# The last 128 output rows of a fused attention and MLP kernel, computed as 384 and then 128 columns

## The chip, the cores and the metric

The kernel runs on one core of a Trainium2 chip. The metric is the device time of one execution in microseconds (us), as the median of several runs. A profiled execution is a separate one: it gives the trace, in which all times count from the first instruction (the span), and it has a time of its own.

## What is computed

The reference is an attention with forget gates, and an MLP on its result:

```python
scores = (q @ k.T) / sqrt(D)                 # per batch and head, S = 576, D = 64
decay  = cum[:, None] - cum[None, :]         # cum: running sum of log(clip(f))
attn   = softmax(where(causal, -1e9, scores + decay))
x      = (attn @ v)                          # heads side by side: 4608 rows of 512
h      = x @ w_in                            # 512 -> 2048
out    = (h - tanh(h)) @ w_out               # 2048 -> 512, float32
```

There are 8 batches of 8 heads. The output is 4608 rows of 512 float32 numbers.

## The kernel before

The work of the attention is cut into 32 pairs of heads. The MLP is cut into NU = 9 row blocks of UW = 512 rows. For each row block there are 32 steps, in a list `mlp` (L429): 16 steps `mlp1` (L386), each of which computes 128 of the 2048 hidden columns for 512 rows and puts them through `gate` (L379), and 16 steps `mlp2` (L413). The order on every engine is written out by hand (`manual_schedule`, L103): `slot` (L456) weaves the MLP's steps in between the attention's, and when the attention is over, L585 runs the steps that are left, one after the other.

`mlp2` multiplies the gated hidden values by `w_out`. Step s handles rows m = s // 4 of the row block (128 rows) and a quarter of the 16 hidden tiles: four matmuls of 128x512 (L419) that accumulate in one PSUM tile `ops`. The tile is taken at the first quarter (L416), from a pool `ps_m` with three buffers, which `gate`'s inputs share. After the fourth quarter, ScalarE copies the 128x512 float32 result from PSUM to an SBUF tile `ost` (L423; pool `tmp`, two buffers), and SP issues one store of 128 rows of 2048 bytes (L425).

So at the very end of the program, TensorE runs 64 matmuls of L419 for four blocks of 128 rows. The last block's copy and store come after the last matmul. The program ends (in the profile, L609) when SP has seen the semaphores of all stores. SP's stores use eight of these semaphores in turn.

The engines touched by the change, with what each still has to do at the end: TensorE only L419; ScalarE only the copies of L423; VectorE nothing after the last `gate` (L383); SP only the stores of L425.

Of the kernel before, what the change touches and what calls it, by code (L numbers as in the profile page):

```python
# [8 lines left out]
FP32 = mybir.dt.float32  # L9
# [13 lines left out]
def kernel(  # L23
# [10 lines left out]
    nc = tc.nc  # L34
    P = 128
# [3 lines left out]
    DM, DFF = moe_w_in.shape  # L39
# [9 lines left out]
    NFT = DFF // P  # L49
    NCH = DM // P  # L50
    UW = 512
    SB = UW // 2
    NU = NT // UW
# [7 lines left out]
    tmp = ctx.enter_context(tc.tile_pool(name="tmp", bufs=2))  # L61
# [4 lines left out]
    ps_m = ctx.enter_context(tc.tile_pool(name="ps_m", bufs=3, space=PSUM))  # L66

    win = wpl.tile([P, NCH, DFF], FP16)
    wout = wpl.tile([P, NFT, DM], FP16)
# [148 lines left out]
    E, XN, GT, M2, AV = {}, {}, {}, {}, {}  # L218
# [167 lines left out]
    def mlp1(u, s):  # L386
# [23 lines left out]
        for m in range(UW // P):  # L410
            GT[(u, s, m)] = gt[:, m * P:(m + 1) * P]

    def mlp2(u, s):  # L413
        m, part = divmod(s, 4)
        if part == 0:
            M2[u] = ps_m.tile([P, DM], FP32, tag="m", name="ops")  # L416
        ops = M2[u]
        for ft in range(part * 4, part * 4 + 4):
            nc.tensor.matmul(out=ops, lhsT=GT[(u, ft, m)], rhs=wout[:, ft, :],  # L419
                             start=(ft == 0), stop=(ft == NFT - 1))  # L420
        if part == 3:
            ost = tmp.tile([P, DM], FP32, tag="ost", name="ost")
            nc.scalar.activation(out=ost, in_=ops, func=AF.Copy)  # L423
            r0 = u * UW + m * P
            nc.sync.dma_start(out=out[r0:r0 + P, :], in_=ost)  # L425

    pairs = [(b, c) for b in range(B) for c in range(NPAIR)]

    mlp = [(fn, u, s) for u in range(NU) for fn in (mlp1, mlp2) for s in range(NFT)]  # L429
    done = [0]  # L430

# [182 lines left out]
```

## Time and profile before

| what | us |
|---|---|
| unprofiled runs: median of 3 (lowest, highest) | 357.48 (357.40, 357.85) |
| the profiled execution's own time | 358.57 |
| its span, first to last instruction | 356.86 |
| TensorE busy | 346.6 (97%) |
| ScalarE busy | 224.5 (63%) |
| VectorE busy | 191.9 (54%) |
| GpSimd busy | 150.9 (42%) |

The profiled execution is 1.71 us longer than its span, and 1.09 us longer than the unprofiled median. The busy times are shares of the whole span, over stages with different limits, so for a change at the end only the last microseconds tell. In the groups of instructions, a line gives the source line, the engine, the operation, what it writes and reads with its shape, the count, then the busy time in us and the mean length of one in ns, and after the second bar the idle time before, with what ended it. In the order of time, a line gives the start and the length in us. Two matmuls that follow each other overlap in these lengths, so their pace is read from the starts.

### The profile page before, as it was taken

How to read it: one execution, taken by the hardware profiler on the slowest of the kernel's cores; microseconds unless marked ns; L12 is line 12 of the kernel's file. 1: busy time of each engine (PE TensorE's matmuls, PEld its weight loads, DVE VectorE, ACT ScalarE, POOL GpSimd, SP SyncE). 2: the span in 40 equal slices, each digit the busy share in tenths (PEclk: the TensorE clock that was granted, in tenths of full speed). 3: DMA queues.
4: the chain of work that ended last, by engine and by line, in shares of the span. 5: the costliest groups of instructions: out<-in, count | busy, mean ns of one | idle time of the engine just before them, and what ended most of it. 6: DMA issues, size and time to landing. Idle time of an engine off the chain costs nothing.

```text
span 356.9 us, 7839 instructions
## 1 busy us (share of the span) xinstructions
PE 346.6 (97%) x2987; PEld 200.9 (56%) x2987; DVE 191.9 (54%) x358; ACT 224.5 (63%) x413; POOL 150.9 (42%) x291
## 2 busy tenths in 40 slices
PE   7989998999999999999999999999999999999995
PEld 3878886555555555555557865555555554444442
DVE  7667788439851676157714681478137513802810
ACT  4686976357855885588657865786568734714721
POOL 8973523554476527662776277632222210000000
PEclk9999999999999999999999999999999999999999
DMA  9999999999199969999999979991220012011002
GB/s 93 144 207 185 206 187 150 133 148 184 24 110 171 144 98 99 154 142 129 69 151 184 119 53 152 156 145 31 85 74 18 15 64 75 2 59 60 2 38 80
DMA packets 148439, 38.70 MB, mean 108 GB/s; under 512 B 137330, under 2 KB 142770, under 8 KB 148402
## 3 DMA queue, kind: packets, MB, share of 16 engines
q0 software_dynamic: 100128, 18.36, 70.2%
q1 hardware_dynamic: 48194, 19.77, 28.5%
q8 instruction: 23, 0.38, 0.4%
q14 instruction: 14, 0.11, 0.1%
q10 hardware_dynamic: 80, 0.08, 0.1%
HBM read 36.85 MB, written 9.44 MB: 130 GB/s over the span
## 4 chain that ended last, share of the span: by engine, by line
PE 92%; ACT 3%; DVE 2%; DMA 1%; issue 1%; ACTq 0%
PE ops L419 35%; PE hps L407 30%; PE ps L332 10%; PE av L360 7%; PE hps L393 3%; PE ps L274 2%; PE t L255 1%; PE av L287 1%; PE t L234 1%; ACT e L279 1%; ACT th L381 1%; ACT e L341 1%; DVE gt L383 1%; DMA lf<-in_f_dram 1%; PE ps L277 1%
## 5 line engine op out<-in xcount | busy, mean ns | idle before, releaser
L419 PE MATMUL ops<-wout,gt 128*128 128x512 f16 x576 | 140.3, 378 | 0.0
L383 DVE TENSOR_TENSOR gt<-hps,th 128x512 f16<-128x512 f32 x144 | 99.1, 690 | 60.3 <-ACT th L381 59.7
L341 ACT ACTIVATE e<-ps 128x512 f16<-128x512 f32 x168 | 99.2, 594 | 47.4 <-PE ps L332 40.0
L407 PE MATMUL hps<-XR,win 128*128 128x512 f16 (+1 forms) x576 | 125.6, 355 | 0.2
L381 ACT ACTIVATE th<-hps 128x512 f32<-128x512 f32 x144 | 86.0, 597 | 29.0 <-PE hps L407 22.9
L351 POOL TENSOR_SCALAR_AFFINE_SELECT e<-e 128x128 f16<-128x128 f16 x144 | 49.0, 340 | 104.6 <-ACT e L341 102.0
L419 PEld LDWEIGHTS <-gt 128*128 128x128 f16 x576 | 51.9, 97 | 52.8
L407 PEld LDWEIGHTS <-win 128*128 128x128 f16 x576 | 52.3, 97 | 44.3 <-issue 0.5
L332 PE MATMUL ps<-QT,KT 67*128 67x512 f16 (+1 forms) x336 | 70.9, 277 | 1.9 <-ACT e L341 1.9
L332 PEld LDWEIGHTS <-KT 67*128 67x128 f16 x336 | 32.8, 98 | 33.4
L423 ACT ACTIVATE ost<-ops 128x512 f32<-128x512 f32 x36 | 21.5, 597 | 39.2 <-PE ops L419 39.2
L366 DVE TENSOR_SCALAR rs<-av 128x10 f32<-128x10 f32 x28 | 4.6, 164 | 68.3 <-PE av L360 68.2
L86 POOL DMA_DIRECT2D vn<-in_v_dram x40 | 34.1, 856 | 9.6 <-PE ps L332 3.6
L360 PEld LDWEIGHTS <-e 128*128 128x128 f16 x784 | 28.1, 97 | 5.5
L360 PE MATMUL av<-vn,e 128*128 128x65 f16 x784 | 29.1, 193 | 0.0
L86 POOL DMA_DIRECT2D qn<-in_q_dram x25 | 21.2, 850 | 10.8 <-PE ps L332 6.2
L368 DVE TENSOR_TENSOR xn<-av,rs 128x640 f16<-128x640 f32 x28 | 23.1, 825 | 1.0
L86 POOL DMA_DIRECT2D kn<-in_k_dram x25 | 21.4, 855 | 1.4 <-issue 1.2
L279 ACT ACTIVATE e<-ps 128x512 f16<-128x512 f32 x25 | 14.4, 596 | 5.3 <-PE ps L277 3.9
L393 PE MATMUL hps<-XR,win 128*128 128x256 f16 x128 | 16.6, 272 | 0.5 <-DVE gt L383 0.5
L243 DVE COPY QT<-t 64x576 f16<-64x576 f16 x12 | 9.6, 803 | 6.8 <-PE t L234 5.2
L274 PE MATMUL ps<-QT,KT 67*128 67x128 f16 (+1 forms) x120 | 11.6, 214 | 1.5 <-ACT e L279 0.8
(79 smaller groups left out, 210.1 us busy)
## 6 DMA issues: line engine op xcount, KB each, us to landing
out_dram<-ost SPq DMA_DIRECT2D x36, 256.0 KB
vn<-in_v_dram POOLq DMA_DIRECT2D x32, 128.0 KB, 5.8
qn<-in_q_dram POOLq DMA_DIRECT2D x24, 128.0 KB, 4.1
kn<-in_k_dram POOLq DMA_DIRECT2D x24, 128.0 KB, 4.5
win<-in_moe_w_in_dram POOLq DMA_DIRECT2D x2, 1024.0 KB, 11.0
wout<-in_moe_w_out_dram POOLq DMA_DIRECT2D x4, 512.0 KB, 11.9
XR<-xn SPq DMA_TRANSPOSE x56
qn<-in_q_dram POOLq DMA_DIRECT2D x1, 576.0 KB, 16.8
```

The lines of the kernel that those rows point to most:

```text
L86: nc.gpsimd.dma_start(out=dst[0:pn, n, h0:h1, 0:D], in_=src[b, h0:h1, n * P:n * P + pn, :].rearrange("h p d -> p h d"))
L332: nc.tensor.matmul(out=ps[:, col:col + n], lhsT=KT[b % 2][0:D + 3, h, j * P:(j + 1) * P], rhs=QT[b % 2][0:D + 3, h, i0:i0 + n], start=True ...
L341: nc.scalar.activation(out=e[:, lo:hi], in_=ps[:, lo:hi], func=AF.Exp, scale=qscale)
L351: nc.gpsimd.affine_select(out=view, in_=view, compare_op=ALU.is_ge, fill=0.0, base=0, pattern=pat, channel_multiplier=-1)
L360: nc.tensor.matmul(out=av[:, a, ib, :], lhsT=E.pop((b, 2 * c + a, j, ib)), rhs=vn[b % 2][:, j, 2 * c + a, 0:D + 1], start=(j == 0), stop=( ...
L368: nc.vector.tensor_tensor(out=xn.rearrange("p i (a d) -> p a i d", a=2), in0=av[:, :, :, 0:D], in1=rs.to_broadcast([P, 2, NJ, D]), op=ALU. ...
L381: nc.scalar.activation(out=th, in_=hps, func=AF.Tanh, scale=-1.0)
L383: nc.vector.tensor_tensor(out=gt, in0=hps, in1=th, op=ALU.add)
L393: nc.tensor.matmul(out=hps[:, w * SB:(w + 1) * SB], lhsT=win[:, ci, ft * P:(ft + 1) * P], rhs=XR[:, ci, t * SB:(t + 1) * SB], start=(ci == ...
L407: nc.tensor.matmul(out=hps[:, o:o + n], lhsT=win[:, ci, s * P:(s + 1) * P], rhs=XR[:, ci, t:t + n], start=(ci == 0), stop=(ci == NCH - 1))
L419: nc.tensor.matmul(out=ops, lhsT=GT[(u, ft, m)], rhs=wout[:, ft, :], start=(ft == 0), stop=(ft == NFT - 1))
L423: nc.scalar.activation(out=ost, in_=ops, func=AF.Copy)
```

## The change

The last block of 128 rows (m = 3 of the last row block) is no longer handled by the four quarters of `mlp2`. A new function computes it at the first of them, and the other three do nothing. It first accumulates columns 0 to 383 over all 16 hidden tiles, copies them with VectorE and stores them, and then does the same for columns 384 to 511. Each part takes its own `ops` and `ost` buffer. The weights of TensorE (the gated tile) are loaded once for each matmul, so 32 times instead of 16. All other blocks are as before.

```diff
+    def last_rows(u, m):
+        r0 = u * UW + m * P
+        for c0, c1 in ((0, 3 * P), (3 * P, DM)):
+            ops = ps_m.tile([P, DM], FP32, tag="m", name="ops")[:, 0:c1 - c0]
+            for ft in range(NFT):
+                nc.tensor.matmul(out=ops, lhsT=GT[(u, ft, m)], rhs=wout[:, ft, c0:c1],
+                                 start=(ft == 0), stop=(ft == NFT - 1))
+            ost = tmp.tile([P, DM], FP32, tag="ost", name="ost")[:, 0:c1 - c0]
+            nc.vector.tensor_copy(out=ost, in_=ops)
+            nc.sync.dma_start(out=out[r0:r0 + P, c0:c1], in_=ost)
+
     def mlp2(u, s):
         m, part = divmod(s, 4)
+        if u == NU - 1 and m == UW // P - 1:
+            if part == 0:
+                last_rows(u, m)
+            return
         if part == 0:
             M2[u] = ps_m.tile([P, DM], FP32, tag="m", name="ops")
```

## The prediction

> **What bounds the kernel now.** I read the page's chain first, then the same chain in order of time over the last 22 us, then the end slice by slice. On the page, TensorE is busy 97% of the span and its clock was granted in full in every slice, so work that ends earlier on another engine is worth nothing unless it stands after the last matmul.
>
> ```profile
> PE   7989998999999999999999999999999999999995
> PEclk9999999999999999999999999999999999999999
> ...
> PE 92%; ACT 3%; DVE 2%; DMA 1%; issue 1%; ACTq 0%
> ```
>
> The change touches only the last rows, so the end of the chain matters (start us, length us, what):
>
> ```profile
> 334.81 4.53 PE hps L407 x21
> 339.34 13.83 PE ops L419 x64
> 353.17 0.03 ACTq L423
> 353.19 0.04 issue
> 353.24 0.60 ACT ost L423
> ```
>
> The reader is to see that TensorE runs its last 64 matmuls without a gap, 13.83 / 64 = 0.216 us each. The last row block is the last 16 of them; by the trace its first starts at 349.53 and its last ends at 353.15. ScalarE then copies the whole 128x512 result, 353.24 to 353.83, alone. SP issues the store at 353.86. The stretches after that show (length, TensorE, weight loads, VectorE, ScalarE, GpSimd, clock, DMA share, GB/s):
>
> ```profile
> 353.20:353.90 0.70, 0.00 (x0) 0.00 (x0) 0.00 (x0) 0.60 (x1) 0.00 (x0) 1.00 0.00 0
> 353.90:354.60 0.70, 0.00 (x0) 0.00 (x0) 0.00 (x0) 0.00 (x0) 0.00 (x0) 1.00 0.00 0
> 354.60:355.60 1.00, 0.00 (x0) 0.00 (x0) 0.00 (x0) 0.00 (x0) 0.00 (x0) 1.00 0.67 262
> 355.60:356.90 1.30, 0.00 (x0) 0.00 (x0) 0.00 (x0) 0.00 (x0) 0.00 (x0) 1.00 0.00 0
> ```
>
> So the 3.70 us after the last matmul are a series: 0.09 handover, 0.60 copy, 0.03 handover, 0.83 from issue to the first packet, 0.83 of packets (354.69 to 355.52), 0.35 until the last count of the store's semaphore (355.87), and 0.99 of closing instructions. SP's waits name that store as what the program's end hangs on:
>
> ```profile
> SPq L609 <- DMA out_dram<-ost: 1.2, 1, 1.2
> ```
>
> All in all the span is 356.86 and the profiled execution 358.57, thus 1.71 outside. The unprofiled median is 357.48 (357.4 to 357.85), 1.09 below the profiled one. I work out a difference inside the span and take it off the median.
>
> **TensorE.** Removed: 16 matmuls of 512 columns. Added: 16 of 384 and then 16 of 128, with 16 more weight loads. No row has 384, so I take the pace from three widths (start, length, then the form):
>
> ```profile
> 18.36 0.39 PE L308 MATMUL x<-id,xn 128*128 128x128 f16 x4
> 18.59 0.22 PE L274 MATMUL ps<-QT,KT 67*128 67x128 f16 x1
> ...
> 27.02 1.04 PE L393 MATMUL hps<-XR,win 128*128 128x256 f16 x8
> 27.90 0.19 PE L274 MATMUL ps<-QT,KT 67*128 67x64 f16 x1
> ```
>
> Starts count, since lengths overlap: (18.59 - 18.36) / 4 = 0.057 at 128 columns (0.0555 as the trace's median), (27.90 - 27.02) / 8 = 0.110 at 256, 0.216 at 512. These lie on a line of 0.0004175 per column plus some 0.002; 384 gives 0.1625. So 16 x (0.1625 + 0.0555) = 3.49 against 16 x 0.216 = 3.46: **0.03 us later**. The last 128-column matmul starts at 349.53 + 16 x 0.1625 + 15 x 0.0555 = 352.97 and lasts 0.22 (the same rows): 353.19. The bounds are 0 and the case in which every weight load (97 ns mean at L419) sets the pace in the narrow pass: 16 x (97 - 55.5) = 0.66. I take the low end, since the 65-column matmuls of L360 start every 29 ns while their weight loads also last 97 ns: loads overlap each other.
>
> Both new accumulations take PSUM buffers that ScalarE emptied at 343.4 and 346.9, so neither waits.
>
> **The copies.** The wide part is ready at 349.53 + 15 x 0.1625 + 0.33 (length between those of 320 and 448 columns, 0.30 and 0.35) = 352.30. VectorE has been idle since 340.7. A float32 copy out of PSUM at these sizes isn't in the trace. The nearest rows are:
>
> ```profile
> L383 DVE TENSOR_TENSOR gt<-hps,th 128x512 f16<-128x512 f32 x144 | 99.1, 690 | 60.3 <-ACT th L381 59.7
> L366 DVE TENSOR_SCALAR rs<-av 128x10 f32<-128x10 f32 x28 | 4.6, 164 | 68.3 <-PE av L360 68.2
> L309 DVE COPY XR<-x 128x512 f16<-128x512 f16 x4 | 1.7, 414 | 0.0
> ```
>
> The two float32 rows give (690 - 164) / 502 = 1.05 ns per column: 0.56 us for 384, 0.29 for 128. By the 2-byte copy (414 at 512 columns, 280 at 256) 128 would be 0.21; the far end is 0.60, as long as today's copy. I take 0.29, from the float32 rows. The wide copy runs 352.39 to 352.94, beside the narrow matmuls. The narrow one is free to start at 353.19 + 0.09 = 353.27, because VectorE has been done 0.33 earlier, and ends at 353.56: 0.27 before today's.
>
> The narrow copy also gains a wait: with two buffers for ost it must wait until the store of the block before last has read its buffer. That store was issued at 350.41 and landed at 352.41, 0.86 before it is needed. Nothing is queued behind the copy on VectorE but the end of the program; SP waits for it.
>
> **The stores.** SP issues the wide store at 352.97, busy 0.33 and then some 0.05 of semaphore work, so it is free at 353.35, before the narrow issue at 353.59. First packets come 0.83 after the issue. A store is 128 packets over 16 engines, 8 each; 2048-byte packets last 84 ns (8 x 84 = 0.67, plus 0.15 of uneven starts = the 0.83 seen). SP's queue has 1024-byte packets of 46 ns and 256-byte ones of 18, though no stores: so 1536 bytes gives 65 and 512 bytes 27. Wide packets run 353.80 to 354.47. Narrow ones could start at 354.42, when most engines are just done: 354.42 + 0.15 + 8 x 0.027 = 354.79. Bounds for 512 bytes: 18 and 84 ns, or -0.07 and +0.46.
>
> Landing 0.35 later gives 355.14 instead of 355.87: 0.73 earlier. After the landing SP goes through its last semaphores at some 0.06 each; the store has moved from the last but one to the last of them, which takes one step off: **0.79 in all**. The terms: -0.31 shorter copy, +0.04 matmuls (0.03 and rounding), -0.46 shorter packets, -0.06 closing step. 357.48 - 0.79 = **356.7 us**, 0.22% less. About 0.2% (0.71 us) is what a measurement of this kernel can tell from no change, so the forecast lies close to that bound.
>
> **Rivals.**
>
> *Weight loads pace the narrow pass.* Each narrow matmul then takes 97 ns, the end comes 0.66 later, and the saving shrinks to 0.13: 357.35. For it: the trace's 128-column runs are only 4 to 8 long. Against it: those runs, and 30 loads in a row at L360 without strain. Chance 0.07. The Trainium skill, page "TensorE: Matmul & The Clock Gate", section "Back-to-back issue gap", speaks for it: in streams of weight load and matmul it states about 81 ns at 128 columns. By that the sum would be 16 x 25 = 0.41 smaller, an estimate of about 357.1; the rows at 56 ns here don't agree, nor does 216 at 512, where it states about 131.
>
> *Small packets cost as much as big ones.* If 512 bytes take 84 ns, the narrow packets follow the wide ones on each engine: 354.47 + 0.67 = 355.14, landed 355.49, closing 0.06: a saving of 0.44, 357.05. For it: time per byte rises from 0.041 ns at 2048 to 0.070 at 256. Against it: 18 ns for 256 bytes shows that no such floor exists on this queue for other transfers. Chance 0.18, partial forms included. The Trainium skill, page "Perfetto Trace Analysis", section "DMA Optimizations", warns that DMAs under 2 KB have significant overhead per transfer, without a figure.
>
> *The second store waits for the first* (the slower side). If the narrow store's first packet can't come before 0.83 after the wide one has landed (354.47 + 0.35 = 354.82), it starts at 355.65, its packets end at 356.02, it lands at 356.37, and the end is 0.44 later than today: 357.9. It decides once the extra delay passes 0.79. Against it: two stores issued at 78.75 and 79.37 landed at 82.25 and 82.94, so the second came 0.68 after the first and not 2. Chance 0.05.
>
> *The split is not what runs.* The built instruction order shows 16 matmuls of 384, 16 of 128, two copies and two stores, last on each engine, and all before unchanged. No chance left.
>
> **How the numbers follow.** The forecast case has the remaining 0.70, with a spread of some 0.25 from the copy, the packets and the three runs; a little over two thirds of that lies beyond 0.71 saved. Faster 0.50, within 0.45, slower 0.05. The range takes in the small-packet case at one end (357.05 and a tenth for the runs) and the low bounds of copy and packets at the other (-0.08, -0.07, and the runs' spread): 356.35 to 357.2.
>
> **What would show it.** Right: the last matmul near 353.2, a copy of 0.29, packets of about 27 ns, a landing near 355.1. Wrong: narrow matmuls above 60 ns apart, packets of 512 bytes near 84 ns, an idle gap between the last matmul and the narrow copy above 0.2 (the ost buffer), or a narrow issue that stands more than 0.05 behind its copy (SP still busy).

## The result and the profile after

The changed kernel takes 356.81 us (median of 22 runs, 356.44 to 358.56) against 357.75 (22 runs, 357.24 to 360.98). The ratio is 0.9974, with a 95% interval of 0.9963 to 0.9985. So it is faster, by 0.93 us as the ratio has it; the interval stays clear of no change, but it reaches across the 0.2% that the prediction named as its bound. By time alone it stays open on which side of that bound the change lies.

The profiled execution of the changed kernel has a span of 354.73 and took 356.44. Its span is 2.13 below that of before, but most of this isn't the change's: 1.39 of it is there by the 12th us, and it then stays at 1.39 in every later stage. The first scores (L274) started between 7.88 and 8.90 in the profiled executions of this study, although nothing ahead of them differs. What the change does is therefore read from the end stretch alone: from the start of ScalarE's copy of the block before last, which all versions have, to the end of the span. Before it is 356.855 - 349.783 = 7.07, after it is 354.728 - 348.394 = 6.33. The difference is **0.74 us**. The landmark in the timeline of the kernel before (start us, length us, engine, line, operation, shapes; in brackets the engine's idle time before it and what ended that):

```profile
349.78 0.60 ACT L423 ACTIVATE ost<-ops 128x512 f32<-128x512 f32 x1 [2.90 <-PE ops L419]
```

The chain of the kernel after, in order of time (start us, length us, what):

```profile
337.95 10.36 PE ops L434 x48
348.31 3.51 PE ops L418 x32
351.81 0.04 DVEq L421
351.85 0.04 issue
351.89 0.29 DVE ost L421
```

TensorE still runs into its last matmul without a gap. The 0.60 of ScalarE that stood behind it has become 0.29 of VectorE. The timeline of the kernel after, in the same stretch:

```profile
348.39 0.60 ACT L438 ACTIVATE ost<-ops 128x512 f32<-128x512 f32 x1 [2.91 <-PE ops L434]
...
351.00 0.56 DVE L421 COPY ost<-ops 128x384 f32<-128x384 f32 x1 [11.70 <-PE ops L418]
351.59 0.96 SPq L422 DMA_DIRECT2D out_dram<-ost  x2
351.89 0.29 DVE L421 COPY ost<-ops 128x128 f32<-128x128 f32 x1 [0.33 <-PE ops L418]
```

The wide copy ends 0.33 before the narrow one starts (the number in brackets is VectorE's idle time, ended by TensorE), so neither the buffer nor the engine holds it up. The kernel before waited for its buffer in the same way, but for a store one block earlier. The two store issues lie in the 0.96 that SP's line merges, at 351.59 and 352.21. Then the transfers (start and end, length, the engines, clock, DMA share, GB/s):

```profile
352.40:353.00 0.60, 0.00 (x0) 0.00 (x0) 0.00 (x0) 0.00 (x0) 0.00 (x0) 1.00 0.87 320
353.00:353.50 0.50, 0.00 (x0) 0.00 (x0) 0.00 (x0) 0.00 (x0) 0.00 (x0) 1.00 0.47 140
353.50:354.70 1.20, 0.00 (x0) 0.00 (x0) 0.00 (x0) 0.00 (x0) 0.00 (x0) 1.00 0.00 0
```

The wide store fills the first of these stretches, and the narrow one follows it directly. SP's waits (total us, how many, the longest) show that the end now hangs on two landings, the wide store's and then the narrow one's:

```profile
SPq L624 <- DMA out_dram<-ost: 0.8, 2, 0.5
```

### The profile page after: what moved, and what is told of

It is laid out like the page before. It is cut to its first block, busy times and chain, and to the rows that moved or that the text cites. A ratio compares the mean times of both kernels' runs of the same rounds, so it can differ in the third digit from the quotient of the medians.

```text
span 354.7 us, 7879 instructions
## 1 busy us (share of the span) xinstructions
PE 345.1 (97%) x3003; PEld 200.5 (57%) x3003; DVE 192.5 (54%) x360; ACT 223.6 (63%) x412; POOL 150.5 (42%) x291
## 4 chain that ended last, share of the span: by engine, by line
PE 92%; ACT 3%; DVE 2%; DMA 1%; issue 1%; ACTq 0%; DVEq 0%
PE ops L434 34%; PE hps L407 30%; PE ps L332 10%; PE av L360 7%; PE hps L393 3%; PE ps L274 2%; PE t L255 1%; PE av L287 1%; PE t L234 1%; PE ops L418 1%; ACT e L279 1%; ACT th L381 1%; ACT e L341 1%; DVE gt L383 1%; DMA lf<-in_f_dram 1%
## 5 line engine op out<-in xcount | busy, mean ns | idle before, releaser
L434 PE MATMUL ops<-wout,gt 128*128 128x512 f16 x560 | 136.8, 378 | 0.0
L434 PEld LDWEIGHTS <-gt 128*128 128x128 f16 x560 | 50.3, 97 | 50.8
L243 DVE COPY KT<-t 64x576 f16<-64x576 f16 x15 | 12.0, 797 | 2.0 <-PE t L234 1.8
```

The lines of the kernel that those rows point to most:

```text
L243: nc.vector.tensor_copy(out=to, in_=of)
```

## The experiments

Most of them change only the last block (L413 to L422 of the changed kernel), and their edits are shown against it. The two runs on the last store's semaphore start from the kernel before. The theory under test is the prediction's: the end is a series of last matmul, copy, issue, packets, landing and closing steps, and the saving is the sum of the terms of the last part. The rivals are that the saving comes from handing the copy to an idle engine, from the copy alone, or from the store alone, and those of the prediction (weight loads set the pace, small packets cost as much as big ones, the second store waits for the first).

### The whole block copied by VectorE

```diff
-        for c0, c1 in ((0, 3 * P), (3 * P, DM)):
+        for c0, c1 in ((0, DM),):
```

> The last block is not split; only its copy moves from ScalarE to VectorE. I read the end stretch: from the start of ScalarE's copy of the block before last to the end of the span (7.07 us before, 6.33 after). Series theory (the end is last matmul + copy + store + closing, and the saving comes from the smaller last part): a 128x512 copy on VectorE takes 0.164 + 502 x 0.00105 = 0.69 against 0.60, end stretch 7.17, time the same as before within 0.2%. Rival 'engine' (the saving comes from handing the last copy to the idle VectorE): end stretch 6.8 or less and a time near that of the change.

Measured: end stretch 7.17, ratio 0.9998 (0.9987 to 1.0009). The group of VectorE in the end stretch:

```profile
L421 DVE COPY ost<-ops 128x512 f32<-128x512 f32 x1 | 0.7, 691 | 12.5 <-PE ops L418 12.5
```

691 ns against ScalarE's 597: the engine isn't what saves, at this size it costs 0.09.

### Split, but copied by ScalarE

```diff
-            nc.vector.tensor_copy(out=ost, in_=ops)
+            nc.scalar.activation(out=ost, in_=ops, func=AF.Copy)
```

> Split as in the change, but both copies stay on ScalarE. Series theory: ScalarE's 128x128 copy takes 0.28 (its 128x128 exponentials take 276 ns), VectorE's took 0.29; end stretch 6.31, time about 0.2 to 0.3% below before, as with the change. Rival 'engine': end stretch near 7.07, time as before.

Measured: end stretch 6.32, ratio 0.9973 (0.9963 to 0.9983). Its timeline:

```profile
351.00 0.49 ACT L421 ACTIVATE ost<-ops 128x384 f32<-128x384 f32 x1 [2.00 <-PE ops L418]
351.52 1.01 SPq L422 DMA_DIRECT2D out_dram<-ost  x2
351.90 0.28 ACT L421 ACTIVATE ost<-ops 128x128 f32<-128x128 f32 x1 [0.40 <-PE ops L418]
```

The same saving without VectorE. The rival "engine" falls.

### Split copies, one store

```diff
+        ost = tmp.tile([P, DM], FP32, tag="ost", name="ost")
         for c0, c1 in ((0, 3 * P), (3 * P, DM)):
...
-            ost = tmp.tile([P, DM], FP32, tag="ost", name="ost")[:, 0:c1 - c0]
-            nc.vector.tensor_copy(out=ost, in_=ops)
-            nc.sync.dma_start(out=out[r0:r0 + P, c0:c1], in_=ost)
+            nc.vector.tensor_copy(out=ost[:, c0:c1], in_=ops)
+        nc.sync.dma_start(out=out[r0:r0 + P, :], in_=ost)
```

> Matmuls and copies split as in the change, both copies into one buffer, and one store of 2048-byte rows after the second. Series theory: only the copy's term is left (0.31 less 0.04 of matmuls), end stretch 7.07 - 0.27 = 6.80, issue to landing 2.0 as before. Rival 'the store alone matters': 7.07 to 7.1. Rival 'the copy alone matters, the smaller store gives nothing': 6.33 to 6.4.

Measured: end stretch 6.76, ratio 0.9988 (0.9976 to 1.0001). The store is issued at 3.76 from the stretch's start and lands at 5.77, 2.00 later, as before. So the split copy alone saves 0.32. Its timeline:

```profile
351.54 0.56 DVE L421 COPY ost<-ops 128x384 f32<-128x384 f32 x1 [11.70 <-PE ops L419]
352.38 0.29 DVE L421 COPY ost<-ops 128x128 f32<-128x128 f32 x1 [0.28 <-PE ops L419]
352.70 0.33 SPq L422 DMA_DIRECT2D out_dram<-ost  x1
```

The stretch is 0.04 shorter than expected, since the narrow copy started 0.04 after the last matmul here, not 0.09 as in the change. In the built order it waits for TensorE's semaphore alone here, and for ScalarE's and those of four earlier stores as well in the change; the last run comes back to this. In the change itself, 0.26 of the 0.74 are there when the last store is issued (3.82 in the stretch against 4.08 before). Of the rest, 0.42 come from the store (1.58 from issue to landing against 2.00) and 0.06 from the closing.

### Cut at 256

```diff
-        for c0, c1 in ((0, 3 * P), (3 * P, DM)):
+        for c0, c1 in ((0, 2 * P), (2 * P, DM)):
```

> The cut moved to 256 and 256. Series theory: last matmul at the same time within 0.02 (16 x 2 x 0.109 = 3.49), last copy 0.42 (+0.13), last packets of 1024 bytes at 46 ns instead of 26 (+0.17): end stretch 6.63. Rival 'a store's packets cost a fixed time, so that it only matters that the store is cut': 6.46. Rival 'the cut does nothing but launch noise': 7.07.

Measured: end stretch 6.58, ratio 0.9983 (0.9975 to 0.9992). The last copy takes 424 ns, the 1024-byte packets 45 ns each. The store takes 1.70 from issue to landing, against 1.58 for 512-byte packets and 2.01 for 2048: a store's time goes with its packets' size, and the rival of a fixed price per packet falls.

### Cut at 448

```diff
-        for c0, c1 in ((0, 3 * P), (3 * P, DM)):
+        for c0, c1 in ((0, 448), (448, DM)):
```

> The cut moved to 448 and 64, both copies on VectorE and both stores on SP. Series theory with queues: narrow matmuls 29 to 31 ns apart, last matmul 0.06 later than with 384/128; but the wide copy (0.62) ends 0.16 after the narrow one could start, so the narrow copy ends 0.17 later although it is short (0.22), and SP is busy with the wide store, so that the narrow issue comes 0.3 later; the narrow packets then queue behind wide ones of 1792 bytes. End stretch 6.65 to 6.75, worse than the change's 6.33. Rival 'the smaller the last part the better': 6.25 or less. If 256-byte packets cost more than the 18 ns of the reads, up to 0.1 more.

Measured: end stretch 6.82, ratio 0.9988 (0.9979 to 0.9997). Its timeline:

```profile
351.64 0.76 DVE L421 COPY ost<-ops 128x448 f32<-128x448 f32 x2 [12.12 <-PE ops L418]
352.29 0.81 SPq L422 DMA_DIRECT2D out_dram<-ost  x2
```

The narrow copy follows the wide one without a gap, so the view shows both as one piece. The narrow part now waits for the wide one on VectorE, on SP (its issue comes 0.32 after the copy has ended, against 0.03 in the change) and in the DMA engines. The last matmul ended at the change's time, not 0.06 later. The stretch is 0.07 above the upper end of what was expected, and the landing alone was 0.10 longer: it came 0.48 after the last 256-byte packet, against 0.38 with the change's 512 bytes, though each packet lasted only 16 ns.

### Cut at 448, the wide part on ScalarE and its own queue

```diff
-        for c0, c1 in ((0, 3 * P), (3 * P, DM)):
+        for c0, c1 in ((0, 448), (448, DM)):
...
-            nc.vector.tensor_copy(out=ost, in_=ops)
-            nc.sync.dma_start(out=out[r0:r0 + P, c0:c1], in_=ost)
+            if c0 == 0:
+                nc.scalar.activation(out=ost, in_=ops, func=AF.Copy)
+                nc.scalar.dma_start(out=out[r0:r0 + P, c0:c1], in_=ost)
+            else:
+                nc.vector.tensor_copy(out=ost, in_=ops)
+                nc.sync.dma_start(out=out[r0:r0 + P, c0:c1], in_=ost)
```

> 448 and 64 again, but the wide part is copied by ScalarE and stored from ScalarE's own queue, so that the narrow copy and issue wait for nothing. Series theory: narrow issue at about the change's time; what is late next is the wide store, whose packets (8 x 75 ns + 0.15) end 0.2 to 0.3 after the change's last packet. End stretch 6.55 to 6.65, between 448/64 on one engine and the change. Rival 'the queues alone made 448/64 bad': 6.25 to 6.3, better than the change.

Measured: end stretch 6.72, ratio 0.9992 (0.9982 to 1.0001). Its timeline:

```profile
351.64 0.54 ACT L422 ACTIVATE ost<-ops 128x448 f32<-128x448 f32 x1 [2.43 <-PE ops L418]
352.11 0.23 DVE L425 COPY ost<-ops 128x64 f32<-128x64 f32 x1 [12.59 <-PE ops L418]
352.21 0.36 ACTq L423 DMA_DIRECT2D out_dram<-ost  x1
352.36 0.33 SPq L426 DMA_DIRECT2D out_dram<-ost  x1
```

The narrow issue is even 0.06 earlier in the stretch than the change's (3.75 against 3.82). Yet its first packet comes 1.31 after the issue instead of 0.85, only when the wide store's packets, issued 0.15 before on the other queue, are nearly through. So freeing the queue and the engine gains only 0.09 on the run before: what is late next is the wide store. Landing was again long, 0.45, and the stretch is 0.07 above the upper end of what was expected. Of the three cuts the change's is near the balance, at which the wide packets end (4.71 in the stretch) just when the narrow ones begin (4.67). No cut between 256 and 384 or between 384 and 448 was run, so the best one isn't known.

### Four parts, two buffers

```diff
-        for c0, c1 in ((0, 3 * P), (3 * P, DM)):
+        for c0, c1 in ((0, P), (P, 2 * P), (2 * P, 3 * P), (3 * P, DM)):
```

> Four parts of 128 columns, with the two ost buffers as they are. Series theory: 64 narrow matmuls at 55.8 ns, last matmul 0.08 later than with the change; but each copy must wait for the landing of the store two before: the second for the store of the block before last, the fourth for the second's, about 1.1 late; and the last store's semaphore is no longer the last in SP's closing order, which adds six steps of 0.062 = 0.37. End stretch about 7.9, slower than before by some 0.2%. Rival 'weight loads pace a long run of narrow matmuls' (81 to 97 ns each): the last matmul 1.6 to 2.6 later.

Measured: end stretch 8.02, ratio 1.0035 (1.0022 to 1.0048). VectorE's waits in the end stretch:

```profile
DVE ost L421 <- PE ops L418: 10.0, 1, 10.0
DVE ost L421 <- DMA out_dram<-ost: 3.2, 2, 1.7
```

Two of the copies waited for a landing, as expected. This is what the wait for a buffer costs when it isn't covered: a buffer comes back only when its store has landed, 1.6 to 2.0 after the issue.

### Four parts, own buffers

```diff
-        for c0, c1 in ((0, 3 * P), (3 * P, DM)):
+        for c0, c1 in ((0, P), (P, 2 * P), (2 * P, 3 * P), (3 * P, DM)):
...
-            ost = tmp.tile([P, DM], FP32, tag="ost", name="ost")[:, 0:c1 - c0]
+            ost = cst.tile([P, P], FP32, tag=f"osl{c0}", name="osl")
```

> Four parts of 128 columns, each with a buffer of its own. Series theory: last matmul 0.08 later than with the change, no wait for a buffer, packets as short as there, and six closing steps (0.37): end stretch 6.33 + 0.08 + 0.37 = 6.78. If the closing term is wrong: 6.41. Rival 'weight loads pace a long run of narrow matmuls': 8 or more.

Measured: end stretch 7.29, ratio 1.0000 (0.9989 to 1.0011), 0.51 longer than expected. The pace isn't the reason; TensorE's timeline in this run gives (3.74 - 0.22) / 63 = 0.0559 per narrow matmul (the last one lasts 0.22), over 64 in a row:

```profile
348.53 3.74 PE L418 MATMUL ops<-wout,gt 128*128 128x128 f16 x64
```

The copies waited for nothing but TensorE. But SP's issues of L422 (shortest, median, longest in ns) hold one of 1336, the third, and the page counts 24 packets of 16384 bytes on the instruction queue instead of 23:

```profile
L422 SPq DMA_DIRECT2D out_dram<-osl x4: 332/358/1336, 349.9 to 353.2; - x4
```

```profile
q8 instruction: 24, 0.39, 0.5%
```

By the trace the 24th packet ran from 351.40 to 352.70, and eight packets of the second store came only after it, up to 1.1 later than the rest. The four parts with two buffers have a 24th packet too, from 352.38 to 353.39. No store's packets ran in that time, and no issue took longer than 383 ns. The next run tests whether it was the cause here.

### Four parts, fewer instructions ahead

This comes on top of the edit of the run before, in `mlp2`. The kernel leaves out half of the sums of four blocks of 128 rows, so its whole time says nothing here.

```diff
-        for ft in range(part * 4, part * 4 + 4):
+        short = u >= NU - 2 and m < 2
+        for ft in range(part * 4, part * 4 + (2 if short else 4)):
...
-                             start=(ft == 0), stop=(ft == NFT - 1))
+                             start=(ft == 0), stop=(ft == (NFT - 3 if short else NFT - 1)))
```

> Four parts of 128 columns with buffers of their own, as in the run before that came out 0.51 later than expected, but with 32 pairs of weight load and matmul left out earlier: in the last two row blocks, the first two blocks of 128 rows sum only 8 of the 16 hidden tiles. TensorE then has as many instructions as with the change. In the four-part run a 24th packet of 16384 bytes on the instruction queue ran during the end stretch, at 2.62, lasted 1.29, and SP's issue of the third store lasted 1.34 instead of 0.33. Theory 'instruction fetch': with fewer instructions there are 23 such packets, none in the end stretch, every store issue lasts 0.33 to 0.38, and the end stretch is the 6.78 first expected. Rival 'four stores in flight are too many for SP's queue': the third or fourth issue is long again and the stretch stays near 7.29.

Measured in one profiled execution: end stretch 6.71, against 6.78 expected and 7.29 in the run before. SP's issues in this run, and the instruction queue on its page:

```profile
L422 SPq DMA_DIRECT2D out_dram<-osl x4: 332/332/333, 344.3 to 347.0; - x4
```

```profile
q8 instruction: 23, 0.38, 0.5%
```

The long issue and the 24th packet are gone together, and with them 0.58. Four stores in flight were not the cause. Why SP's third issue became long while eight packets of the second store were held up isn't shown.

### The last store's semaphore

Both edits are to the kernel before. The one of the first run is shown; the second has a 3 in the place of the 2.

```diff
-            nc.sync.dma_start(out=out[r0:r0 + P, :], in_=ost)
+            for _ in range(2 if (u, m) == (NU - 2, 0) else 1):
+                nc.sync.dma_start(out=out[r0:r0 + P, :], in_=ost)
```

> The kernel before, with the first store of the last row block but one issued twice. Nothing at the end changes but which of the eight semaphores the last store uses: the last in SP's closing order instead of the last but one. Closing theory (each semaphore that SP still has to look at after the last landing costs 0.06): end stretch 7.07 - 0.06 = 7.01. Otherwise 7.07.

> The same with that store issued three times, so that the last store uses the first semaphore in SP's closing order, and six more semaphores follow it than before. Closing theory: 7.07 + 6 x 0.062 = 7.44. Otherwise 7.07.

Measured in one profiled execution each: 7.02 and 7.46, against 7.01 and 7.44 expected. For the second, with a span of 356.44, the copy of the block before last in the timeline is

```profile
348.98 0.60 ACT L423 ACTIVATE ost<-ops 128x512 f32<-128x512 f32 x1 [2.91 <-PE ops L419]
```

From the last landing to the end it takes 0.93 when the last store's semaphore is the last that SP looks at, 0.99 when one follows, 1.30 with six (the four-part runs) and 1.37 with seven (the last of these two): 0.06 for each. The whole times of these two runs, 360.19 and 358.14, say nothing on this. In the first, ScalarE's instructions stood 1.68 later than in the profile before from the 61st us on, over 250 us ahead of the extra store.

### Own buffers, copied by ScalarE

```diff
-            ost = tmp.tile([P, DM], FP32, tag="ost", name="ost")[:, 0:c1 - c0]
-            nc.vector.tensor_copy(out=ost, in_=ops)
+            ost = cst.tile([P, c1 - c0], FP32, tag=f"osl{c0}", name="osl")
+            nc.scalar.activation(out=ost, in_=ops, func=AF.Copy)
```

> Cut at 384, both copies on ScalarE, and a buffer of its own for each part, so that each copy waits for TensorE's semaphore alone. With shared buffers the narrow copy started 0.09 after the last matmul, in the runs in which it waits for no store 0.04. Theory 'each further semaphore to look at costs handover time': narrow copy and issue 0.05 earlier than in the split copied by ScalarE (6.32), end stretch 6.27 if the wide store's packets are through by then, else up to 6.32. Rival 'the 0.04 comes from VectorE alone': 6.32. By time it can't be told from the change: ratio to before 0.997.

Measured: end stretch 6.27, ratio 0.9963 (0.9947 to 0.9978). The narrow copy starts 0.04 after the last matmul (3.445 against 3.408 in the stretch), as theory has it, on ScalarE too. In the timeline:

```profile
352.89 0.28 ACT L421 ACTIVATE osl<-ops 128x128 f32<-128x128 f32 x1 [0.40 <-PE ops L418]
```

It has the shortest end of all versions with the kernel's full work, 0.07 below the change's. Its ratio overlaps the change's, so by time the two can't be told apart.

## Why the prediction was right

The forecast was 356.7, 0.79 less than before; the end stretch lost 0.74 and the medians differ by 0.94. That 356.7 lies only 0.11 from the measured 356.81 is in part luck: the median before was 357.75 over 22 runs and not the 357.48 of the three runs that the forecast started from, and the medians differ by 0.15 more than forecast. The two errors work against each other. What bears the forecast out is the end stretch, step by step, times in us:

| step | predicted | measured |
|---|---|---|
| last matmul later | 0.03 | 0.04 |
| last copy, from 0.60 to | 0.29 | 0.292 |
| narrow issue, against the issue before | -0.27 | -0.26 |
| issue to first packet | 0.83 | 0.85 |
| narrow packets, first start to last end | 0.37 | 0.35 |
| 512-byte packet, ns | 27 | 26.5 |
| landing after the last packet | 0.35 | 0.38 |
| closing | -0.06 | -0.06 |

- **The matmuls.** Linear interpolation between three widths held: 0.1625 per matmul at 384 columns, and 0.0559 at 128. The rival in which weight loads pace the narrow pass is refuted by the group of 64 narrow matmuls in a row. The Trainium skill, page "TensorE: Matmul & The Clock Gate", section "Back-to-back issue gap", states about 81 ns at 128 columns in such streams; 64 pairs at 55.9 ns here don't agree.
- **The copy.** The two float32 rows were the right neighbours; the 2-byte copy, with its shorter time per column, would have been wrong.
- **The packets.** The price per packet of SP's queue, read from transfers of another kind, held for stores: 16, 26.5, 45, 65, 74 and 84 ns for 256, 512, 1024, 1536, 1792 and 2048 bytes. The rival in which small packets cost as much as big ones is refuted by this row and by the cut at 256.
- **The second store.** It didn't wait for the first to land: its first packet came at 4.67 in the stretch and the first store landed at 5.06. It started just as the first one's packets ran out (4.71), as the prediction had it.
- **The copy's wait for its buffer.** It was covered, as the prediction had it. That the copy gains a wait isn't right as it stands: the last copy of the kernel before waits for a buffer as well, and the change makes the store that it waits for a later one.
- **The split as such.** The split without VectorE saves as much as the change, VectorE without the split saves nothing, and the split copy with a single store saves 0.32.

What was off by the most is small: issue to first packet and landing took 0.05 more together than taken over from the big store. The difference between 0.74 in the trace and 0.94 in the medians lies within the interval of the ratio (0.54 to 1.32 of 357.75), and no run here assigns it to anything. In every version that was run repeatedly, the change of the end stretch, as a share of the whole time, lies within the interval of the ratio. So whether the time fell by more than the 0.71 of the bound, to which the prediction gave about even chances, the runs don't decide.

## What to carry to other kernels

When the last matmul ends late and everything behind it is a series, the last part's size sets the length of that series. A cut paid here as long as the part ahead of it was out of every queue (copy engine, issuing queue, DMA engines) when the small part arrived. A first guess at the cut is the one at which the big part's packets end as the small part's start; that rule rests on three cuts. With the smallest last part that was run (64 columns), more than half of the gain was lost again. Where executions differ by a microsecond at their start, measure such a change from a landmark shortly ahead of it.

## What was not expected of the hardware

- A packet of 16384 bytes on the instruction queue, which lasts 0.9 to 1.8 us, can fall into the end stretch when 64 instructions are added to TensorE's. It did in both four-part runs with that many. In one of them it cost 0.5 to 0.6 us, with a store's packets and the issue of the next store held up; in the other no store's packets met it. The Trainium skill, page "Runtime: NRT & Kernel Launch", section "Instruction fetch mechanics", speaks of refills in blocks of 16 KiB whose cost is mostly hidden; this one was not hidden, and no run here shows what the 23 others cost.
- The stores of 256-byte packets landed 0.48 and 0.45 after their last packet, against 0.35 to 0.39 for the last stores of 512 bytes and more. The size need not be the cause. In the same two runs the 1792-byte store, whose packets still ran when the 256-byte ones began, landed late too, by 0.44 and 0.41. So did the first 512-byte store of the four-part runs, which began while 2048-byte packets ran: 0.41 to 0.42. No run has a store of 256 bytes that stands alone.
- Further semaphores to look at show. After the last landing each one costs 0.06. Between the last matmul and the copy they cost 0.05 (0.09 against 0.04), and as much with four stores' semaphores on VectorE as with one on ScalarE (beside ScalarE's own in both), so there the price isn't one for each.
- A store on another queue didn't overtake: narrow packets from SP's queue began only 0.14 before the end of the wide ones, whose store ScalarE's queue had issued 0.15 before; with the change's 0.85 from issue to first packet they would have begun 0.46 earlier, an estimate.
